# Sorting the values of batches 1 to 3 as rows in four array tiles, by way of DRAM

## The chip, the cores and the metric

The kernel runs on one core of one Trainium2 chip. The metric is the time of one execution on the device in microseconds (us), the median of several runs. The core has TensorE (PE in the profile; its weight loads are PEld), VectorE (DVE), ScalarE (ACT), GpSimd (POOL), SyncE (SP), and 16 DMA engines that all queues share.

## The reference

Sorted attention over blocks, then a feed-forward network. There are 4 batches, 8 heads, 768 positions, 64 values per head; a sequence has 8 blocks of 96.

```python
P = sort_net                                   # [4, 8, 8, 8]
for _ in range(5):
    P = exp(P - max(P, -1));  P = P / (sum(P, -1) + 1e-9);  P = P / (sum(P, -2) + 1e-9)
k_sorted = einsum('bhij,bhjcd->bhicd', P, k_b) # k in blocks: j, position c in the block, d
v_sorted = einsum('bhij,bhjcd->bhicd', P, v_b)
attn = softmax(q_b @ k_sorted.T / 8)           # each block of q against its own sorted block
x = (attn @ v_sorted), heads side by side      # [3072, 512]
r = maximum(x @ w_in, 0)                       # w_in [512, 2048]
out = (s * r * r + b) @ w_out                  # w_out [2048, 512]
```

## The kernel before

Work goes by batch. A batch has two tiles (halves) of 384 tokens for the feed-forward part. `ffn1(t)` computes the hidden layer of tile t: eight steps, each with 8 matmuls of 384 columns (`hps`, L408) into a pair of PSUM banks, a ReLU on ScalarE (`rt`, L422) and a square on VectorE (`gt`, L423). `ffn2(t)` computes the output: three groups of 128 tokens, each with 16 matmuls of 512 columns (`ops`, L433), then scale and bias on VectorE (`ot`, L454) and a store from SP's queue (L457). A fourth of such a group, four matmuls, is a slot; after each slot other work can be put in by a dictionary, `slots`, so the order on TensorE is written out by hand. A tile has 12 slots, 0 to 11.

The attention of batch n = b + 1 is put between the matmuls of `ffn2` of batch b. Its pieces are `K` (`k_piece`, `tp`, L252: sorted keys), `V` (`v_piece`, `tv`, L302: sorted values), `SC` (`s_piece`, `sc`, L317: scores, with the exponential to `at` on ScalarE), `P` (`p_piece`, `pv`, L352: weighted values, divided on VectorE into `x`) and `TD` (`t_dma`, L389: transpose of `x` into `xt` by DMA from SP's queue, for the next `ffn1`). Each piece takes a pair of PSUM banks from a pool of three (`psa`). `q_dma` (L294) transposes the queries by DMA from SP's queue, in two halves of 4 blocks.

The two halves z of a block's 48 positions each lie on rows of their own: a raw tile has a partition for each (head h, block j, half z), and on it 48 positions of 64 values. The sort is a matmul over (h, j, z) with the matrix `PD` (the entries of P, masked). For the scores the sorted keys must have d on the partitions, which comes out of the matmul if the raw data are the stationary operand. For the weighted values the sorted values (`VS`) must have the positions c on the partitions: `v_piece` takes for each d the raw values of 48 positions (filled up to 64) as the stationary operand, and `PD` for one half z as the moving one. To have the 48 positions side by side, the raw values are first copied with c and d exchanged (`VP`): by ScalarE for batch 0, by eight GpSimd copies for the later batches (`v_sort`, L171). So each later batch has 4 pieces with 32 matmuls of 64 columns each:

```python
nc.tensor.matmul(out=ps[z * GAP:(z + 1) * GAP, d, :],
                 lhsT=VP[b % 2][:, d0 + d, :], rhs=PD[b][:, :, z, :],
                 start=True, stop=True)
```

The loads of batch n+1 (`loads`: k, v, then eight DMAs for q, and `v_sort`) are issued on GpSimd's queue; for batch 1 after the loads of the weights, for batches 2 and 3 behind a small copy (`gate`, L558) that waits for the first square of `ffn1` of the batch before. Batch 0's attention and the five rounds of normalising `sort_net` run ahead of all this, up to about 24 us; `ffn1` of batch 0 starts there.

Of the kernel before, what the change touches and what calls it, by code (L numbers as in the profile page):

```python
# [22 lines left out]
def kernel(  # L23
# [32 lines left out]

    raw = [t.rearrange("b h (j z c) d -> b (h j z) (c d)", j=NB, z=2) for t in (q, k, v)]

    const = ctx.enter_context(tc.tile_pool(name="const", bufs=1))
    rawp = ctx.enter_context(tc.tile_pool(name="rawp", bufs=2))  # L60
    trp = ctx.enter_context(tc.tile_pool(name="trp", bufs=2))
# [5 lines left out]
    osb = ctx.enter_context(tc.tile_pool(name="osb", bufs=3))  # L67
    psa = ctx.enter_context(tc.tile_pool(name="psa", bufs=3, space=bass.MemoryType.PSUM))
    psb = ctx.enter_context(tc.tile_pool(name="psb", bufs=2, space=bass.MemoryType.PSUM))
    ctx.enter_context(tc.manual_schedule())  # L70


# [11 lines left out]
    def load(t, b, parts=1):  # L84
        ti = rawp.tile([128, C2, D], BF, tag=f"raw{t}", name=f"raw{t}")
        RAW[t, b] = ti
        n = C2 // parts
        for c in range(0, C2, n):
            nc.gpsimd.dma_start(out=ti[:, c:c + n, :].rearrange("p c d -> p (c d)"),
                                in_=raw["qkv".index(t)][b][:, c * D:(c + n) * D])  # L90

    QTOK = {}

    def load_q(b, ns=range(NB)):
# [4 lines left out]
        for n in ns:  # L99
# [5 lines left out]
    VP = [const.tile([128, D, GAP], BF, name=f"vp{i}") for i in range(2)]  # L105
    KS = [const.tile([128, NG, 2, GAP], BF, name=f"ks{i}") for i in range(2)]
    VS = [const.tile([KR, 2 * NG, VW], BF, name=f"vs{i}") for i in range(2)]
    nc.vector.memset(VP[0][:, :, C2:GAP], 0.0)
    nc.vector.memset(KS[0][:, :, :, C2:GAP], 0.0)
    nc.vector.memset(sne[:, NB, :], 1e-9)  # L110

# [3 lines left out]
    idv = ident.rearrange("p (a e j z) -> p a e j z", a=NHP, e=2, j=NB)  # L115
    emat = const.tile([BH, B, 128], FP)
    nc.gpsimd.memset(emat, 0.0)
    nc.gpsimd.affine_select(out=emat, in_=emat, pattern=[[-H, B], [-1, H], [0, 2 * NB]], base=0,
                            channel_multiplier=1, compare_op=ALU.not_equal, fill=1.0)
    load("k", 0, 3)  # L120
    load_q(0, range(HB))
# [27 lines left out]
    def fill_vs(i):  # L149
        nc.gpsimd.memset(VS[i][:, :, D:VW], 1.0)  # L150
        nc.gpsimd.memset(VS[i][32:GAP, :, D:VW], 0.0)
        nc.gpsimd.memset(VS[i][32:C2, :, D:VW], 1.0)

    fill_vs(0)
    Z = []

    def warm(n, w=512):
# [4 lines left out]
                             start=True, stop=True)  # L162


    def permute(eng, b, src, cs=slice(0, C2), ds=slice(0, D)):
        o = VP[b % 2][:, ds, cs]
        i = src[:, cs, ds].rearrange("p c d -> p d c")
        if eng is nc.scalar:
            eng.copy(out=o, in_=i)
        else:  # L170
            eng.tensor_copy(out=o, in_=i)  # L171


    rstat = const.tile([BH, NB], FP)
    rrec = const.tile([BH, NB], FP)
    jsel = const.tile([128, NB], FP)
    bm = const.tile([128, 2 * 2 * NHP], FP)
    idle = [
        lambda: nc.vector.tensor_reduce(
            out=jsel, in_=ident.rearrange("p (h j z) -> p j h z", h=H, j=NB), axis=AX.XY, op=ALU.add),  # L180
# [8 lines left out]
    for it in range(5):  # L189
        nc.scalar.activation(out=sn, in_=sn, func=AF.Exp)  # L190
        if it >= 1:
            permute(nc.scalar, 0, v0f, slice((it - 1) * CV, it * CV))
# [7 lines left out]
        nc.vector.tensor_reduce(out=rstat, in_=sne.rearrange("p i j -> p j i"),  # L200
                                axis=AX.X, op=ALU.add)
# [17 lines left out]
    def take_p(b0, n, pe):  # L219

        bs = slice(b0, b0 + n)
        tmp = rtp.tile([128, n * NB, NB], FP, tag=f"tmp{n}", name="tmp")
        nc.vector.tensor_tensor(out=tmp, in0=pe.rearrange("p b i j -> p (b i) j"),
                                in1=spread(jsel, [[0, n * NB], list(jsel.ap[1])]), op=ALU.mult)
        nc.vector.tensor_reduce(out=PT[:, bs].rearrange("p b i -> p (b i)"), in_=tmp, axis=AX.X,
                                op=ALU.add)
        cs = rtp.tile([128, n], FP, tag=f"cs{n}", name="cs")
        nc.vector.tensor_reduce(out=cs, in_=PT[:, bs], axis=AX.X, op=ALU.add)
        nc.vector.reciprocal(out=RC[:, bs], in_=cs)

    def build_pd(b):
        pd = const.tile([128, 2, 2, NG], BF, name=f"pd{b}")
        nc.vector.scalar_tensor_tensor(
            out=pd.rearrange("p e z (a i) -> p (e z a) i", i=NB),
            in0=spread(bm, [list(bm.ap[1]), [0, NB]]), scalar=RC[:, b:b + 1],
            in1=spread(PT[:, b], [[0, 4 * NHP], list(PT.ap[2])]), op0=ALU.mult, op1=ALU.mult)
        PD[b] = pd

    def evac(eng, out, in_):
        if eng == "A":  # L240
# [50 lines left out]
    def q_dma(b):  # L291
        qt = q_tile(b)
        for n0 in (0, HB):
            nc.sync.dma_start_transpose(  # L294
                out=qt[:, n0:n0 + HB].rearrange("p n a t -> p (n a) t"),
                in_=QTOK[b][:, n0:n0 + HB].rearrange("p n h d -> p (n h d)"))

    def v_piece(b, d0, eng):
        ps = psa.tile([128, CK, 2 * NG], FP, tag="a", name="tv")
        for d in range(CK):  # L300
            for z in range(2):
                nc.tensor.matmul(out=ps[z * GAP:(z + 1) * GAP, d, :],  # L302
                                 lhsT=VP[b % 2][:, d0 + d, :], rhs=PD[b][:, :, z, :],
                                 start=True, stop=True)
        evac(eng, VS[b % 2][:, :, d0:d0 + CK], ps[0:KR].rearrange("p d g -> p g d"))

# [150 lines left out]
        nc.sync.dma_start(out=out[r0:r0 + 128, ns], in_=ot[:, ns])  # L457


    take_p(0, 1, spread_p(0, 1))  # L460
    build_pd(0)

    nc.gpsimd.tensor_copy(out=ones[:, 0:1], in_=PD[0][:, 0, 0, 0:1])
# [31 lines left out]
    nc.gpsimd.memset(sel, 0.0)  # L495
    for r in range(0, 128, 32):
        nc.gpsimd.memset(sel[r:r + 1], 1.0)
    nc.gpsimd.memset(VP[1][:, :, C2:GAP], 0.0)
    nc.gpsimd.memset(KS[1][:, :, :, C2:GAP], 0.0)
    fill_vs(1)  # L500
    for t, src in ((s_bc, moe_s), (b_bc, moe_b)):
        nc.gpsimd.dma_start(out=t, in_=src.to_broadcast([128, 1]))

    def v_sort(b):
        for i in range(8):
            permute(nc.gpsimd, b, RAW["v", b], ds=slice(i * 8, (i + 1) * 8))

    def loads(b):
        load("k", b)
        load("v", b)  # L510
        load_q(b)
        v_sort(b)

    loads(1)

# [22 lines left out]
    def V(b, i, eng): return lambda: v_piece(b, i * CK, eng)  # L538
# [73 lines left out]
```

## Time and profile before

| | |
|---|---|
| median of 3 runs | 228.4 us (228.14 to 228.75) |
| profiled execution | 228.41 us, span 226.6 us, granted clock 1.00 |
| TensorE busy | 218.9 us |
| VectorE, ScalarE, GpSimd busy | 124.5, 99.5, 68.2 us |
| `hps` and `ops` (L408, L433) | 85.7 us each |
| `tv` (L302), all batches | 512 matmuls, 10.0 us busy |
| GpSimd copies to `VP` (L171) | 24, 19.0 us |
| `vs<-tv` out of PSUM | VectorE 1222 ns, ScalarE 1019 ns each |
| DMA packets | 53930; 44944 of them under 512 bytes |
| q's loads | 32 DMAs, 96 KB each, 9.5 us to landing |

A row of the groups reads: line, engine, operation, output <- input, partitions x elements and type, x count, then busy time, mean ns of one and idle time ahead of it with what ended it. A matmul's duration has its way through the array in it, so the distance of two is shorter than the duration of one. The chain in order of time gives start, length and what ran. In a line of DMA queues the numbers are packets, MB and the packets' time as a share of 16 engines; the share can be over 100%, since packets overlap.

### The profile page before, as it was taken

How to read it: one execution, taken by the hardware profiler on the slowest of the kernel's cores; microseconds unless marked ns; L12 is line 12 of the kernel's file. 1: busy time of each engine (PE TensorE's matmuls, PEld its weight loads, DVE VectorE, ACT ScalarE, POOL GpSimd, SP SyncE). 2: the span in 40 equal slices, each digit the busy share in tenths (PEclk: the TensorE clock that was granted, in tenths of full speed). 3: DMA queues.
4: the chain of work that ended last, by engine and by line, in shares of the span. 5: the costliest groups of instructions: out<-in, count | busy, mean ns of one | idle time of the engine just before them, and what ended most of it. 6: DMA issues, size and time to landing. Idle time of an engine off the chain costs nothing.

```text
span 226.6 us, 5806 instructions
## 1 busy us (share of the span) xinstructions
PE 218.9 (97%) x2542; PEld 133.2 (59%) x2542; DVE 124.5 (55%) x223; ACT 99.5 (44%) x128; POOL 68.2 (30%) x112
## 2 busy tenths in 40 slices
PE   7996999999999999999999999999999999999993
PEld 8985656655555556665555556655566566654452
DVE  6766467553647634498656634498557543441121
ACT  4966476564325225637143236627152246550000
POOL 8467797338400009291000028490000000000000
PEclk9999999999999999999999999999999999999999
DMA  5999999999711558993112459991123240001212
GB/s 190 238 105 133 181 164 206 207 196 136 164 49 49 129 151 136 188 166 72 49 47 73 138 120 176 176 171 36 49 95 67 100 114 0 4 0 46 94 49 93
DMA packets 53930, 25.82 MB, mean 114 GB/s; under 512 B 44944, under 2 KB 49296, under 8 KB 53904
## 3 DMA queue, kind: packets, MB, share of 16 engines
q0 software_dynamic: 30864, 12.85, 47.1%
q1 hardware_dynamic: 23040, 12.59, 20.9%
q8 instruction: 20, 0.33, 0.6%
q14 instruction: 6, 0.05, 0.1%
HBM read 27.27 MB, written 6.29 MB: 148 GB/s over the span
## 4 chain that ended last, share of the span: by engine, by line
PE 86%; DVE 5%; DMA 3%; POOL 2%; ACT 1%; issue 1%; POOLq 0%
PE ops L433 36%; PE hps L408 36%; PE pv L352 3%; PE tv L302 3%; DMA qtok<-in_q_dram 3%; PE sc L317 2%; PE tp L252 2%; PE ops L446 2%; POOL wi L131 1%; DMA sne<-in_sort_net_dram 1%; ACT rt L422 1%; POOL qtok L100 1%; ACT sne L190 1%; PE scb L332 1%; DVE rstat L200 0%
## 5 line engine op out<-in xcount | busy, mean ns | idle before, releaser
L408 PE MATMUL hps<-xt,wi 128*128 128x384 bf16 x512 | 85.7, 326 | 0.3 <-DMA qtok<-in_q_dram 0.3
L433 PE MATMUL ops<-wo,gt 128*128 128x512 bf16 x368 | 85.7, 379 | 0.0
L422 ACT ACTIVATE rt<-hps 128x768 bf16<-128x768 f32 x64 | 51.1, 811 | 53.4 <-PE hps L408 45.6
L423 DVE TENSOR_TENSOR gt<-rt 128x768 bf16<-128x768 bf16 x64 | 46.9, 739 | 41.2 <-ACT rt L422 40.4
L408 PEld LDWEIGHTS <-wi 128*128 128x128 bf16 x512 | 49.3, 98 | 33.5 <-issue 0.6
L433 PEld LDWEIGHTS <-gt 128*128 128x128 bf16 x368 | 33.7, 98 | 36.9 <-issue 0.6
L454 DVE SCALAR_TENSOR_TENSOR ot<-ops,s_bc,bias 128x512 f32<-128x512 f32 (+1 forms) x25 | 18.2, 730 | 30.8 <-PE ops L433 28.2
L322 ACT ACTIVATE at<-sc 112x768 bf16<-112x768 f32 x28 | 21.3, 808 | 30.3 <-PE sc L317 30.3
L100 POOL DMA_DIRECT2D qtok<-in_q_dram x32 | 24.9, 793 | 18.4 <-DMA rawv<-in_v_dram 9.0
L360 DVE TENSOR_TENSOR x<-pv,rec 96x512 bf16<-96x512 f32 x32 | 22.0, 687 | 1.1
L243 DVE CAST vs<-tv 112x1024 bf16<-112x1024 f32 x11 | 13.2, 1222 | 10.8 <-PE tv L302 10.7
L171 POOL COPY vp<-rawv 128x384 bf16<-128x384 bf16 x24 | 19.0, 849 | 0.0
L558 POOL COPY gate<-gt 128x1 bf16<-128x1 bf16 x2 | 0.4, 193 | 56.6 <-DVE gt L423 56.6
L352 PEld LDWEIGHTS <-at 112*128 112x128 bf16 (+1 forms) x256 | 12.8, 101 | 7.2 <-ACT at L322 1.1
L352 PE MATMUL pv<-vs,at 112*128 112x66 bf16 (+1 forms) x256 | 13.9, 195 | 1.0 <-DVE vs L243 1.0
L161 PE MATMUL z<-zeros 128*128 128x140 bf16 (+1 forms) x132 | 11.7, 256 | 1.2 <-DVE zeros L104 1.2
L302 PEld LDWEIGHTS <-vp 128*64 128x64 bf16 x512 | 9.0, 113 | 3.9 <-issue 3.6
L161 PEld LDWEIGHTS <-zeros 128*128 128x128 bf16 x132 | 10.1, 111 | 1.4 <-DVE zeros L103 1.0
L302 PE MATMUL tv<-pd,vp 128*64 128x64 bf16 x512 | 10.0, 197 | 0.9 <-issue 0.8
L241 ACT CAST ks<-tp 128x1024 bf16<-128x1024 f32 x8 | 8.1, 1012 | 4.0 <-PE tp L252 3.9
L131 POOL DMA_DIRECT2D wi<-in_moe_w_in_dram x16 | 8.6, 552 | 2.6 <-DMA wi<-in_moe_w_in_dram 0.9
L241 ACT CAST vs<-tv 112x1024 bf16<-112x1024 f32 x5 | 5.1, 1019 | 9.3 <-PE tv L302 9.3
(76 smaller groups left out, 104.3 us busy)
## 6 DMA issues: line engine op xcount, KB each, us to landing
out_dram<-ot SPq DMA_DIRECT2D x23, 256.0 KB, 2.0
qtok<-in_q_dram POOLq DMA_DIRECT2D x32, 96.0 KB, 9.5
rawk<-in_k_dram POOLq DMA_DIRECT2D x3, 768.0 KB, 6.8
rawv<-in_v_dram POOLq DMA_DIRECT2D x3, 768.0 KB, 10.0
wi<-in_moe_w_in_dram POOLq DMA_DIRECT2D x16, 128.0 KB, 5.2
wo<-in_moe_w_out_dram POOLq DMA_DIRECT2D x4, 512.0 KB, 10.8
v0f<-in_v_dram SPq DMA_DIRECT2D x4, 384.0 KB, 4.3
rawk<-in_k_dram POOLq DMA_DIRECT2D x3, 256.0 KB, 7.9
```

The source lines that it names most:

```text
L100: nc.gpsimd.dma_start(out=QTOK[b][:, n], in_=qv[:, n])
L161: nc.tensor.matmul(out=Z[0][:, 0:w], lhsT=zeros[:, 0:128], rhs=zeros[:, 0:w], start=True, stop=True)
L171: eng.tensor_copy(out=o, in_=i)
L302: nc.tensor.matmul(out=ps[z * GAP:(z + 1) * GAP, d, :], lhsT=VP[b % 2][:, d0 + d, :], rhs=PD[b][:, :, z, :], start=True, stop=True)
L322: nc.scalar.activation(out=at, in_=sc[0:KR, :, 0:TG], func=AF.Exp, scale=scale)
L352: nc.tensor.matmul(out=pv[0:m, e, n * VW:(n + 1) * VW], lhsT=atf[:, c0:c0 + m], rhs=VS[b % 2][:, e * NG + g0 + n, :], start=True, stop=True)
L360: nc.vector.tensor_tensor(out=x[:, :, hp * 128:(hp + 1) * 128].rearrange("p n (e d) -> p e n d", e=2), in0=pvv[:, :, :, 0:D], in1=rec.unsq ...
L408: nc.tensor.matmul(out=H1[i][:, f, 0:TG], lhsT=wi[:, hp, fc:fc + 128], rhs=xt[:, :, hp, :], start=(hp == 0), stop=(hp == NHP - 1))
L422: nc.scalar.activation(out=rt, in_=h, func=AF.Relu)
L423: nc.vector.tensor_tensor(out=gt[:, 2 * i:2 * i + 2, :], in0=rt, in1=rt, op=ALU.mult)
L433: nc.tensor.matmul(out=ops, lhsT=gt[:, f, m * 128:(m + 1) * 128], rhs=wo[:, f, :], start=(f == 0), stop=(f == NF - 1))
L454: nc.vector.scalar_tensor_tensor(out=ot[:, ns], in0=ops, scalar=s_bc, in1=BIAS[0][:, ns], op0=ALU.mult, op1=ALU.add)
```

## The change

For batches 1 to 3, `v_piece` and the GpSimd copies go. The raw k and v tiles of these batches get the order (z, h, j) on the partitions, each loaded by two DMAs of 64 partitions. A new `v_rows` takes a small matrix `PV` (64 rows of one half z by 64 sorted (e, a, i)) as the stationary operand and the raw values themselves, eight positions of 64 values, as the moving one: for each of two parities y of the position and two halves z, one matmul in one of four 64 x 64 tiles of the array. Three pieces of four matmuls make a batch. The result has (y, head and block) on the partitions and the positions along them, the wrong way round for the weighted values. So it goes to a DRAM tile `DV` as rows (48 positions of each half z by 64 sorted heads and blocks, 64 bf16 values = 128 bytes apiece), by two DMAs per piece on SP's queue, and comes back by `v_back`, two DMAs on GpSimd's queue, into `VS` with the positions on the partitions. Masks for the new order are made in `ffn1(1)`.

In the slots, V moves from 5 and 9 to 0 of the first tile, with `v_back` behind it; K from 2 to 3; the scores of the first half from 9 and 11 to 10 and 11; the weighted values of the first half from slot 11 on, one at a time, to slots 3 and 5 of the second tile, in pairs; its transpose from 2 to 5; the second half likewise follows in pairs, its transpose in slot 10 in place of 8. For batch 1, `q_dma` comes behind V in place of ahead of `ffn2`. Half of the filling of `emat` comes later in GpSimd's order.

```diff
+    def load_z(t, b):
+        ti = rawp.tile([128, C2, D], BF, tag=f"raw{t}", name=f"raw{t}")
+        RAW[t, b] = ti
+        for z in range(2):
+            nc.gpsimd.dma_start(out=ti[z * 64:(z + 1) * 64].rearrange("p c d -> p (c d)"),
+                                in_=rawz["qkv".index(t)][b, z])
...
+    DV = drp.tile([BLK, 2 * NG, D], BF, name="dv")
+    VO = const.tile([128, 2, C2 // 2, D], BF)
...
-    nc.gpsimd.affine_select(out=emat, in_=emat, pattern=[[-H, B], [-1, H], [0, 2 * NB]], base=0,
+    nc.gpsimd.affine_select(out=emat[:, 0], in_=emat[:, 0], pattern=[[-1, H], [0, 2 * NB]], base=0,
...
+    def masks_z():
+        idz = ident.rearrange("p (z a e j) -> p z a e j", z=2, a=NHP, e=2)
+        nc.vector.tensor_reduce(
+            out=jselz, in_=ident.rearrange("p (z h j) -> p j z h", z=2, h=H), axis=AX.XY, op=ALU.add)
+        nc.vector.tensor_reduce(
+            out=bmz.rearrange("p (e z a) -> p e z a", e=2, z=2),
+            in_=idz.rearrange("p z a e j -> p e z a j"), axis=AX.X, op=ALU.add)
+        bv = bmz.rearrange("p (e z a) -> p e z a", e=2, z=2)
+        nc.vector.tensor_tensor(out=bmv.rearrange("p (e a) -> p e a", e=2), in0=bv[:, :, 0],
+                                in1=bv[:, :, 1], op=ALU.add)
...
     def build_pd(b):
+        PD[b] = build(b, bmz if b else bm, "pd").rearrange("p (e z a) i -> p e z (a i)", e=2, z=2)
+        if b:
+            PV[b] = build(b, bmv, "pv").rearrange("p m i -> p (m i)")
...
+    def v_rows(b, i, eng):
+        src, n = RAW["v", b], 8
+        ps = psa.tile([128, 2, n, D], FP, tag="a", name="vo")
+        for y in range(2):
+            for z in range(2):
+                zs, ys = slice(z * 64, (z + 1) * 64), slice(y * 64, (y + 1) * 64)
+                c0 = i * 2 * n + y
+                nc.tensor.matmul(out=ps[ys, z], lhsT=PV[b][zs], rhs=src[zs, c0:c0 + 2 * n - 1:2, :],
+                                 start=True, stop=True, tile_position=(z * 64, y * 64))
+        vo = VO[:, :, i * n:(i + 1) * n, :]
+        evac(eng, vo.rearrange("p z c d -> p z (c d)"), ps.rearrange("p z c d -> p z (c d)"))
+        dv = DV.rearrange("(z t c y) g w -> z t (y g) c w", z=2, y=2, c=n)
+        for z in range(2):
+            nc.sync.dma_start(out=dv[z, i], in_=vo[:, z])
+
+    def v_back(b):
+        for z in range(2):
+            nc.gpsimd.dma_start(out=VS[b % 2][z * GAP:z * GAP + C2, :, 0:D],
+                                in_=DV[z * C2:(z + 1) * C2])
...
-    def v_sort(b):
-        for i in range(8):
-            permute(nc.gpsimd, b, RAW["v", b], ds=slice(i * 8, (i + 1) * 8))
...
     def loads(b):
-        load("k", b)
-        load("v", b)
+        load_z("v", b)
+        load_z("k", b)
         load_q(b)
-        v_sort(b)
...
-    ffn1(1, {-2: [TP(0, 1, 2, "D")], 1: [lambda: take_p(1, B - 1, PB), PDB(1)], 4: [PDB(2)],
+    ffn1(1, {-2: [TP(0, 1, 2, "D")], 1: [masks_z, lambda: take_p(1, B - 1, PB, jselz), PDB(1)], 4: [PDB(2)],
...
-        q_dma(n)
+        if b:
+            q_dma(n)
         s0 = {
-            2: [K(n, 0, "A"), K(n, 1, "D"), K(n, 2, "A")],
-            5: [V(n, 0, "D"), V(n, 1, "A"), V(n, 2, "D")],
-            9: [V(n, 3, "D"), SC(n, 0, 0), SC(n, 0, 1)],
-            11: [P(n, 0, 0), SC(n, 0, 2), SC(n, 0, 3)]}
+            0: [V(n, 0, "D"), V(n, 1, "A"), V(n, 2, "D"), lambda: v_back(n)]
+               + ([] if b else [lambda: q_dma(n)]),
+            3: [K(n, 0, "A"), K(n, 1, "D"), K(n, 2, "A")],
+            10: [SC(n, 0, 0), SC(n, 0, 1)],
+            11: [SC(n, 0, 2), SC(n, 0, 3)]}
         ffn2(2 * b, s0)
-        ffn2(2 * b + 1, {0: [P(n, 0, 1)], 1: [P(n, 0, 2)],
-                         2: [P(n, 0, 3), TD(n, 0), SC(n, 1, 0), SC(n, 1, 1)],
-                         4: [P(n, 1, 0)], 5: [P(n, 1, 1), SC(n, 1, 2), SC(n, 1, 3)],
-                         7: [P(n, 1, 2)], 8: [P(n, 1, 3), TD(n, 1)]})
+        ffn2(2 * b + 1, {3: [P(n, 0, 0), P(n, 0, 1)],
+                         5: [P(n, 0, 2), P(n, 0, 3), TD(n, 0)],
+                         6: [SC(n, 1, 0), SC(n, 1, 1)], 7: [SC(n, 1, 2), SC(n, 1, 3)],
+                         8: [P(n, 1, 0), P(n, 1, 1)],
+                         10: [P(n, 1, 2), P(n, 1, 3), TD(n, 1)]})
```

More of the change, by code (lines that the diff above doesn't have):

```diff
@@ L57 @@
     raw = [t.rearrange("b h (j z c) d -> b (h j z) (c d)", j=NB, z=2) for t in (q, k, v)]
+    rawz = [t.rearrange("b h (j z c) d -> b z (h j) (c d)", j=NB, z=2) for t in (q, k, v)]
     const = ctx.enter_context(tc.tile_pool(name="const", bufs=1))
@@ L69 @@
     psb = ctx.enter_context(tc.tile_pool(name="psb", bufs=2, space=bass.MemoryType.PSUM))
+    drp = ctx.enter_context(tc.tile_pool(name="drp", bufs=1, space=bass.MemoryType.DRAM))
     ctx.enter_context(tc.manual_schedule())
@@ L104 @@
     nc.vector.memset(zeros[:, 128:512], 0.0)
-    VP = [const.tile([128, D, GAP], BF, name=f"vp{i}") for i in range(2)]
+    VP = const.tile([128, D, GAP], BF)
     KS = [const.tile([128, NG, 2, GAP], BF, name=f"ks{i}") for i in range(2)]
     VS = [const.tile([KR, 2 * NG, VW], BF, name=f"vs{i}") for i in range(2)]
-    nc.vector.memset(VP[0][:, :, C2:GAP], 0.0)
+    DV = drp.tile([BLK, 2 * NG, D], BF, name="dv")
+    VO = const.tile([128, 2, C2 // 2, D], BF)
+    nc.vector.memset(VP[:, :, C2:GAP], 0.0)
     nc.vector.memset(KS[0][:, :, :, C2:GAP], 0.0)
@@ L147, in load_w @@
             nc.gpsimd.dma_start(out=wo[:, fs, :], in_=wov[:, fs, :])
[L149 to L154, printed above, removed]
+    nc.gpsimd.memset(VS[0][:, :, D:VW], 1.0)
+    nc.gpsimd.memset(VS[0][32:GAP, :, D:VW], 0.0)
+    nc.gpsimd.memset(VS[0][32:C2, :, D:VW], 1.0)
+    for z in range(2):
+        em = emat[:, 1:B, z * 64:(z + 1) * 64]
+        nc.gpsimd.affine_select(out=em, in_=em, pattern=[[-H, B - 1], [-1, H], [0, NB]], base=-H,
+                                channel_multiplier=1, compare_op=ALU.not_equal, fill=1.0)
     Z = []
@@ L162, in warm, with permute @@
                              start=True, stop=True)
[L165 to L171, printed above, removed]
+    def permute(cs):
+        nc.scalar.copy(out=VP[:, :, cs], in_=v0f[:, cs, :].rearrange("p c d -> p d c"))
     rstat = const.tile([BH, NB], FP)
@@ L177 @@
     bm = const.tile([128, 2 * 2 * NHP], FP)
+    jselz = const.tile([128, NB], FP)
+    bmz = const.tile([128, 2 * 2 * NHP], FP)
+    bmv = const.tile([128, 2 * NHP], FP)
     idle = [
@@ L191 @@
         if it >= 1:
-            permute(nc.scalar, 0, v0f, slice((it - 1) * CV, it * CV))
+            permute(slice((it - 1) * CV, it * CV))
         if it in (1, 2):
@@ L217, in spread_p, with take_p @@
         return pe
-    def take_p(b0, n, pe):
+    def masks_z():
[8 more added lines that the diff above has]
+                                in1=bv[:, :, 1], op=ALU.add)
+    def take_p(b0, n, pe, sel):
         bs = slice(b0, b0 + n)
@@ L223, in take_p @@
         nc.vector.tensor_tensor(out=tmp, in0=pe.rearrange("p b i j -> p (b i) j"),
-                                in1=spread(jsel, [[0, n * NB], list(jsel.ap[1])]), op=ALU.mult)
+                                in1=spread(sel, [[0, n * NB], list(sel.ap[1])]), op=ALU.mult)
         nc.vector.tensor_reduce(out=PT[:, bs].rearrange("p b i -> p (b i)"), in_=tmp, axis=AX.X,
@@ L229, in take_p, with build @@
         nc.vector.reciprocal(out=RC[:, bs], in_=cs)
-    def build_pd(b):
[L232 to L237, printed above, removed]
+    PV = {}
+    def build(b, m, name):
+        n = m.shape[1]
+        pd = const.tile([128, n, NB], BF, name=f"{name}{b}")
+        nc.vector.scalar_tensor_tensor(
+            out=pd, in0=spread(m, [list(m.ap[1]), [0, NB]]), scalar=RC[:, b:b + 1],
+            in1=spread(PT[:, b], [[0, n], list(PT.ap[2])]), op0=ALU.mult, op1=ALU.mult)
+        return pd
+    def build_pd(b):
+        PD[b] = build(b, bmz if b else bm, "pd").rearrange("p (e z a) i -> p e z (a i)", e=2, z=2)
+        if b:
+            PV[b] = build(b, bmv, "pv").rearrange("p m i -> p (m i)")
     def evac(eng, out, in_):
@@ L296, in q_dma @@
                 in_=QTOK[b][:, n0:n0 + HB].rearrange("p n h d -> p (n h d)"))
+    def v_rows(b, i, eng):
[13 more added lines that the diff above has]
+    def v_back(b):
+        for z in range(2):
+            nc.gpsimd.dma_start(out=VS[b % 2][z * GAP:z * GAP + C2, :, 0:D],
+                                in_=DV[z * C2:(z + 1) * C2])
     def v_piece(b, d0, eng):
@@ L302, in v_piece @@
                 nc.tensor.matmul(out=ps[z * GAP:(z + 1) * GAP, d, :],
-                                 lhsT=VP[b % 2][:, d0 + d, :], rhs=PD[b][:, :, z, :],
+                                 lhsT=VP[:, d0 + d, :], rhs=PD[b][:, :, z, :],
                                  start=True, stop=True)
@@ L457, in store @@
         nc.sync.dma_start(out=out[r0:r0 + 128, ns], in_=ot[:, ns])
-    take_p(0, 1, spread_p(0, 1))
+    take_p(0, 1, spread_p(0, 1), jsel)
     build_pd(0)
@@ L497 @@
         nc.gpsimd.memset(sel[r:r + 1], 1.0)
-    nc.gpsimd.memset(VP[1][:, :, C2:GAP], 0.0)
     nc.gpsimd.memset(KS[1][:, :, :, C2:GAP], 0.0)
-    fill_vs(1)
+    nc.gpsimd.memset(VS[1][:, :, D:VW], 1.0)
+    nc.gpsimd.memset(VS[1][32:GAP], 0.0)
+    nc.gpsimd.memset(VS[1][32:C2, :, D:VW], 1.0)
     for t, src in ((s_bc, moe_s), (b_bc, moe_b)):
         nc.gpsimd.dma_start(out=t, in_=src.to_broadcast([128, 1]))
-    def v_sort(b):
-        for i in range(8):
-            permute(nc.gpsimd, b, RAW["v", b], ds=slice(i * 8, (i + 1) * 8))
     def loads(b):
-        load("k", b)
-        load("v", b)
+        load_z("v", b)
+        load_z("k", b)
         load_q(b)
-        v_sort(b)
     loads(1)
@@ L537, in K, with V @@
     def K(b, i, eng): return lambda: k_piece(b, i * CK, eng)
-    def V(b, i, eng): return lambda: v_piece(b, i * CK, eng)
+    def V(b, i, eng): return lambda: v_rows(b, i, eng)
     def SC(b, h, i): return lambda: s_piece(b, h, i)
```

## The prediction

> **What bounds the kernel now.** I read the busy table first, then the chain that ended last, by line and in order of time, then the DMA views, because the change adds DMA.
>
> ```profile
> PE 218.9 (97%) x2542; PEld 133.2 (59%) x2542; DVE 124.5 (55%) x223; ACT 99.5 (44%) x128; POOL 68.2 (30%) x112
> ...
> PE 86%; DVE 5%; DMA 3%; POOL 2%; ACT 1%; issue 1%; POOLq 0%
> PE ops L433 36%; PE hps L408 36%; PE pv L352 3%; PE tv L302 3%; DMA qtok<-in_q_dram 3%; PE sc L317 2%; PE tp L252 2%; PE ops L446 2%; POOL wi L131 1%; DMA sne<-in_sort_net_dram 1%; ACT rt L422 1%; POOL qtok L100 1%; ACT sne L190 1%; PE scb L332 1%; DVE rstat L200 0%
> ```
>
> TensorE works 97% of the span and the chain is TensorE's own work: from 52 us on it has no wait. What is taken off TensorE there shortens the run by as much, and a wait put in front of it lengthens it by as much. In order of time, the stage of batch 2 and, above it, one row from the stage before:
>
> ```profile
> 47.75 0.98 PE cps L527 x16
> ...
> 102.30 2.59 PE ops L433 x12
> 104.89 1.64 PE tp L252 x96
> 106.53 2.70 PE ops L433 x12
> 109.23 1.64 PE tv L302 x96
> 110.86 3.56 PE ops L433 x16
> 114.42 0.63 PE tv L302 x32
> 115.05 0.45 PE sc L317 x16
> 115.49 1.83 PE ops L433 x8
> 117.33 0.27 PE pv L352 x8
> ```
>
> A slot is four `ops` matmuls, 2.59/3 = 0.863 us. The sort of the values (`tv`) takes 1.64 + 0.63 = 2.27 us per batch.
>
> **Removed from TensorE:** three times 2.27 = 6.8 us (batch 0 keeps its sort). **Put in its place:** 12 matmuls of 64 rows by 64 columns with 512 moving columns per batch. The trace has no such tile, but it has the two halves of it: `cps` puts 16 matmuls of 512 columns in four column tiles into 0.98 us, 61 ns each where `ops` takes 216 ns, so four column tiles run at once; `sc` puts 16 matmuls of 96 columns in two row tiles into 0.45 us, 28 ns each, where 96 columns at `ops`' rate (512 in 216 ns) take 40 ns, so row tiles overlap too. Bounds: 12 x 61 ns = 0.74 us, and 12 x 216 ns = 2.59 us. I take 0.74, since `cps` has the same columns. Saving: 3 x (2.27 - 0.74) = **4.6 us**. The K, score and weighted-value matmuls keep their number; pairing them only moves them.
>
> The Trainium skill ("TensorEngine Tiling (Array Packing)", Key Properties) says that a change of tiling mode drains the array; the group after a change takes 2.70 instead of 2.59 us here. Both kernels change in and out of tiles at each group, so by the rule as by the row the sum moves by under 0.2 us a batch.
>
> **Removed elsewhere, worth nothing:** 24 GpSimd copies (19.0 us, 849 ns each). While they run, one `gt` operation of VectorE stretches to some 4 us (ScalarE waits 3.97 us at 103.2), but `hps` keeps its 20.80 us per 128 matmuls, as TensorE has three PSUM buffers ahead. One of four evacuations per batch also goes. **Added on VectorE** in the second FFN tile: two mask reductions (0.27 us by the `bm` row), one small product, three further builds (0.35 us by the `pd` row), at most 1.8 us over several steps. They delay squares, and three `rt` buffers at 1.3 us a step (3.9 us) cover that; uncovered it would cost about 1 us. The split `emat` select runs in GpSimd's 4.8 us wait for `pd`. Loading k and v in two halves moves the same bytes.
>
> **The round trip through DRAM** decides. Per batch SP issues 6 stores of 1024 pieces of 128 bytes, and GpSimd, once they have landed, 2 loads of 3072 pieces; the first weighted values wait for the loads. Behind the stores on SP's queue stand the output stores, and in the first turn the two transposes of q. Behind the loads on GpSimd's queue stand only loads for later. No store of 128-byte pieces to DRAM is in the trace. The nearest rows: one microsecond full of q's load (256 bytes read, 128 written), and one full of SP's transposes (256-byte packets out of SBUF):
>
> ```profile
> q0 software_dynamic: 1223, 0.15, 241.1%
> ```
>
> ```profile
> q1 hardware_dynamic: 830, 0.21, 115.2%
> ```
>
> So 0.82 us per 1000 packets in the first and 1.20 us in the second. The first is nearer in size, the second in queue and source; I take the middle, 1.01 us per 1000, 6.2 us for 6144. Times below count from the start of the first `ops` group of a stage (102.30 above).
>
> - Stores: slot 0 ends at 0.9, the first piece's matmuls at 1.1 and, with a tail of 0.2 us (an `ops` matmul lasts 379 ns at 216 ns spacing), at 1.3. VectorE is free of the last `gt` (ScalarE 0.81, VectorE 0.56) at 1.4. The evacuation takes 1.22 us (`vs<-tv`), so the first store goes at 2.7 and the third piece's at 3.9. An output store lands 2.0 us after issue with some 0.7 us of data, so 1.3 us go by around it; from the transposes I take 1.3 us ahead of the data and 0.5 us after it. Data: 4.0 to 10.2, last landing 10.7; the first half's last store lands 1.0 us earlier, at 9.7. SP's issuing (0.33 us for an output store, 1.44 us for a transpose of 1536 packets, so up to 1.0 us for 1024 pieces) ends at 8.7 at the latest and lies beside the data.
> - Loads: issuing costs GpSimd 779 ns at 768 pieces (q) and 566 ns at 128 (k, v), 0.33 ns a piece, so 0.52 + 3072 x 0.33 ns = 1.5 us (in plain proportion 3.1). Then 1.3 us to first data, 6144 pieces at q's rate 5.0 us, and 1.0 us to landing. From 9.7: **18.5 us**. Bounds: with half of q's bytes read per piece 2.5 us less, with issue in proportion 2.2 us more.
> - Needed: slot 3 of the second tile, after 16 slots (13.8 us), sort 0.7, K 1.6, four scores 1.8 and 0.3 for changes of mode: **18.3 us**. The move from slot 11 of the first tile to there is the cover; without those four slots the wait would be 3.5 us longer.
>
> So TensorE waits 0.2 us in each of the last two stages. In the first stage the transposes of q follow the stores: 10.2 + 1536 packets at 830/us (1.9) + 0.5 = 12.6, against scores due at slot 10: 11 x 0.863 + 0.7 + 1.6 + 0.2 = 12.0. That is 0.6 us of wait, which also gives the values their time. Waits: 0.6 + 0.2 + 0.2 = **1.0 us**. What comes later keeps a margin: the transpose of the first half (x) starts at slot 5 and has 6 slots and other work, 8.6 us, for some 2 us of normalising and 3.7 us to land. An output tile has three buffers, so 12 slots of 0.86 us pass before one is wanted again.
>
> **Sum:** the profiled execution took 228.41 us (span 226.6), which is the median of the runs (228.4). 228.4 - 4.6 + 1.0 = **224.8 us**.
>
> A rule of the Trainium skill speaks against the change: "DMA: Bandwidth & Descriptors", Specifications, says that transfers under 512 bytes are read, modified and written. Read so, each stored piece would move twice, 12.4 us in place of 6.2, and by it the time would be about 243 us. The same page ("Why small descriptors are slow") counts, for a packet, one cycle per 32 bytes plus 3, which for 128 bytes is an estimate of 8 ns per engine, 3.2 us for the stores, and the time 223.8 us. The q row has 128-byte writes, to SBUF, that are not slowed in that way; no run shows it for DRAM.
>
> **Rivals.**
>
> *Fully hidden, 223.8 us.* The stores go at q's rate (5.0 us) or the loads at half its time; then both waits vanish. For it: q's load is bound by twice the bytes per piece. Chance 0.17.
>
> *Slower: the stores' landing.* Every microsecond d that they take beyond 6.2 us is paid three times, as the stage has no slack left at slot 3. The waits are 1.0 + 3d, and pass the 4.6 us saved at d = 1.2 us, that is from 7.4 us for 6144 pieces, 830 per us: just the transposes' rate. At 600 per us (10.2 us, d = 4.0) the time is 223.8 + 13.0 = 236.8 us; at 400 (15.4 us, d = 9.2) it is 252.4 us. For it: SP's only measured rate for small packets is the point of balance, and writing DRAM in small pieces has no row. Against it: output stores of 2 KB land in 2.0 us. The return leg too can add d. Chance 0.38, of which 0.06 lie within 0.7 us of no change.
>
> *The four tiles do not overlap.* Then the sort takes 2.59 us, 0.3 more than now: 228.4 + 1.0 + 1.0 = 230.4 us. Against it are `cps` and `sc`; that no row has both kinds of tile at once is for it. Chance 0.07.
>
> *Forecast:* almost hidden, 224.3 to 227.6, chance 0.36. That leaves 0.02 for a cause not seen, counted as slower.
>
> **Numbers.** No change means within 0.3%, 0.7 us, about what a measurement of this kernel can tell. Faster: 0.36 + 0.17 = 0.53; same 0.06; slower 0.32 + 0.07 + 0.02 = 0.41. The range goes from 223.4 (hidden, and a little of the tiles' overlap better than counted) to 240, where the stores run at about 540 per us; I leave 0.14 above it and 0.03 below. The forecast's own range is 224.3 to 227.6.
>
> **What would show it.** In the chain after: `vo` groups of about 0.7 us where `tv` had 2.27; a wait of `pv` for the DMA of `vs` of about 0.2 us in the last two stages, and of `sc` for `qt` of about 0.6 us in the first; `dv` stores landing about 8 us after the first issue. A wait of `pv` over 1.5 us per stage, or `vo` over 1.5 us, would make the forecast wrong, the first by the rate of the stores or of the loads, which the packets per microsecond on the two queues tell apart.

## The result, and the profile after

The changed kernel takes 250.79 us (median of 4 runs, 249.47 to 253.03), the kernel before beside it 228.27 us: a ratio of 1.099 (95% interval 1.091 to 1.108), 22.5 us slower. The forecast was 224.8 us, 3.5 us faster.

From the page of the changed kernel, the busy times and the chain that ended last, by engine and line (span 249.3 us):

```profile
PE 220.6 (88%) x2194; PEld 128.4 (51%) x2194; DVE 110.0 (44%) x226; ACT 99.5 (40%) x128; POOL 63.3 (25%) x101
...
PE 63%; DMA 21%; DVE 6%; issue 3%; SPq 2%; ACT 2%; POOLq 0%; POOL 0%; DVEq 0%
PE hps L462 33%; PE ops L487 19%; DMA vs<-dv 15%; DMA dv<-VO 5%; PE pv L406 4%; SPq L344 2%; PE ops L500 1%; PE sc L371 1%; PE tv L356 1%; DVE VO L275 1%; ACT rt L476 1%; DMA sne<-in_sort_net_dram 1%; ACT sne L202 1%; PE z L175 1%; DVE vs L275 0%
```

Where the kernel before had 86% of its chain on TensorE and 3% on DMA, a fifth of it is now DMA, most of it the loads back (`vs<-dv`). TensorE's busy time did not fall, although 348 matmuls are gone. The chain in order of time for the stage of batch 2 shows the turn of it:

```profile
113.02 0.86 PE ops L487 x4
113.88 0.77 PE vo L338 x12
114.65 2.71 PE ops L487 x12
...
118.02 4.86 DMA dv<-VO
...
124.91 10.75 DMA vs<-dv
...
135.79 1.09 PE pv L406 x16
136.89 3.41 PE ops L487 x8
```

`vo` takes 0.77 us where `tv` had 2.27. The stage begins at 113.0. The stores land at 122.9, 9.9 us into it. The second load back, issued at 124.9, lands at 135.66. The two lines after it are slow too: `pv` takes 1.09 us where two pieces had 0.54, and eight `ops` matmuls 3.41 where they had 1.73. The timeline of TensorE gives the wait ahead of `pv` in brackets:

```profile
80.59 1.09 PE L406 MATMUL pv<-vs,at 112*128 112x66 bf16 x16 [10.22 <-DMA vs<-dv]
135.79 1.09 PE L406 MATMUL pv<-vs,at 112*128 112x66 bf16 x16 [5.24 <-DMA vs<-dv]
192.11 1.09 PE L406 MATMUL pv<-vs,at 112*128 112x66 bf16 x16 [5.02 <-DMA vs<-dv]
```

And the busy times by stretch (columns: length, then busy time of PE, PEld, DVE, ACT and POOL, then the granted clock, the DMA share and GB/s) show why the work after a wait is slow:

```profile
131.00:138.00 7.00, 2.21 (x20) 1.41 (x21) 1.82 (x5) 0.00 (x0) 0.00 (x0) 0.76 0.67 107
138.00:140.00 2.00, 2.00 (x6) 0.72 (x5) 0.22 (x1) 0.00 (x0) 0.00 (x0) 0.50 0.00 0
140.00:142.00 2.00, 2.00 (x21) 1.28 (x19) 1.12 (x4) 0.00 (x0) 0.00 (x0) 0.65 0.00 0
142.00:150.00 8.00, 8.00 (x95) 4.58 (x94) 5.28 (x11) 2.99 (x4) 0.00 (x0) 1.00 0.36 84
```

During the wait the granted clock falls to 0.50, and it is back at 1.00 only some time after TensorE has work again: 2.8 us in the first stage, 5.6 in the second and 4 in the third. So the account is: saved on the sort 3 x (2.27 - 0.77) = 4.5 us; waits of `pv` 10.2 + 5.2 + 5.0 = 20.4; a wait of the scores 0.3; and from the first `pv` of a stage to the next hidden layer 11.6, 13.0 and 12.2 us, where the same work adds up to 10.2 us at full clock, so 6.2 us. Together 26.9 - 4.5 = 22.4 us.

### The profile page after: what moved, and what is told of

Same layout as the page of the kernel before. It is cut to its first block, busy times and chain, and to the rows that moved or that the text cites. A ratio compares the mean times of both kernels' runs of the same rounds, so it can differ in the third digit from the quotient of the medians.

```text
span 249.3 us, 5152 instructions
## 1 busy us (share of the span) xinstructions
PE 220.6 (88%) x2194; PEld 128.4 (51%) x2194; DVE 110.0 (44%) x226; ACT 99.5 (40%) x128; POOL 63.3 (25%) x101
## 4 chain that ended last, share of the span: by engine, by line
PE 63%; DMA 21%; DVE 6%; issue 3%; SPq 2%; ACT 2%; POOLq 0%; POOL 0%; DVEq 0%
PE hps L462 33%; PE ops L487 19%; DMA vs<-dv 15%; DMA dv<-VO 5%; PE pv L406 4%; SPq L344 2%; PE ops L500 1%; PE sc L371 1%; PE tv L356 1%; DVE VO L275 1%; ACT rt L476 1%; DMA sne<-in_sort_net_dram 1%; ACT sne L202 1%; PE z L175 1%; DVE vs L275 0%
## 5 line engine op out<-in xcount | busy, mean ns | idle before, releaser
L487 PE MATMUL ops<-wo,gt 128*128 128x512 bf16 x368 | 89.5, 393 | 0.0
L487 PEld LDWEIGHTS <-gt 128*128 128x128 bf16 x368 | 35.0, 101 | 41.4 <-issue 5.9
L477 DVE TENSOR_TENSOR gt<-rt 128x768 bf16<-128x768 bf16 x64 | 35.5, 558 | 45.4 <-ACT rt L476 45.1
L349 POOL DMA_DIRECT2D vs<-dv x6 | 8.0, 1341 | 39.6 <-DMA dv<-VO 39.6
L413 DVE RECIPROCAL rec<-pv 96x8 f32<-96x8 f32 x32 | 6.3, 198 | 20.9 <-PE pv L406 20.9
L175 PE MATMUL z<-zeros 128*128 128x140 bf16 (+1 forms) x132 | 11.6, 254 | 1.2 <-DVE zeros L114 1.2
L371 PEld LDWEIGHTS <-ks 64*128 64x128 bf16 x224 | 5.2, 94 | 5.7 <-issue 4.1
L371 PE MATMUL sc<-qt,ks 64*128 64x96 bf16 x224 | 7.4, 204 | 0.4 <-DMA qt<-qtok 0.3
L275 DVE CAST VO<-vo 128x1024 bf16<-128x1024 f32 x6 | 7.1, 1217 | 0.7 <-PE vo L338 0.7
## 6 DMA issues: line engine op xcount, KB each, us to landing
wo<-in_moe_w_out_dram POOLq DMA_DIRECT2D x4, 512.0 KB, 11.2
```

What stands on the lines that cost most here:

```text
L175: nc.tensor.matmul(out=Z[0][:, 0:w], lhsT=zeros[:, 0:128], rhs=zeros[:, 0:w], start=True, stop=True)
L275: nc.vector.tensor_copy(out=out, in_=in_)
L371: nc.tensor.matmul(out=sc[:, e, n * BLK:(n + 1) * BLK], lhsT=KS[b % 2][pr, g0 + n].rearrange("p z c -> p (z c)"), rhs=QT[b][pr, half * HB ...
L477: nc.vector.tensor_tensor(out=gt[:, 2 * i:2 * i + 2, :], in0=rt, in1=rt, op=ALU.mult)
L487: nc.tensor.matmul(out=ops, lhsT=gt[:, f, m * 128:(m + 1) * 128], rhs=wo[:, f, :], start=(f == 0), stop=(f == NF - 1))
```

## The experiments

The theory after the first look was that only the return leg is wrong: all else is the gain that was forecast. The rivals for why it is long were the uneven addresses of its pieces (A), GpSimd's queue (B), other transfers beside it (C), the number of small pieces (D), a slow source (E), and that a load reaches 48 partitions of one half of SBUF alone (F).

**No loads back.**

```diff
-            0: [V(n, 0, "D"), V(n, 1, "A"), V(n, 2, "D"), lambda: v_back(n)]
+            0: [V(n, 0, "D"), V(n, 1, "A"), V(n, 2, "D")]
```

> Leaves out the loads back from DRAM: the weighted values of batches 1 to 3 read values that were never brought in. Theory (the return leg is what is late, all else is a gain): no wait of pv for the DMA of vs, no fall of TensorE's clock, and the sort's saving stands alone, 228.3 - 3 x (2.27 - 0.77) = 223.8 us; the wait of the scores for qt in the first stage (0.3 us) may stay, so 223.5 to 224.5. Rival (the four tiles, the stores or the new slots cost something themselves): over 226 us.

Measured: 225.14 us against 229.11 for the kernel before beside it, ratio 0.980 (0.974 to 0.986). Everything but the return leg is worth 4 us. In its profile the scores of the first stage wait 2.5 us for `qt`, more than the 0.3 expected, and a little over a microsecond after the wait the granted clock goes down (last column but two):

```profile
66.21 0.72 PE L371 MATMUL sc<-qt,ks 64*128 64x96 bf16 x16 [2.50 <-DMA qt<-qtok]
```

```profile
67.00:68.00 1.00, 1.00 (x4) 0.20 (x2) 0.00 (x0) 1.00 (x2) 0.00 (x0) 0.78 1.15 317
68.00:69.00 1.00, 1.00 (x18) 0.74 (x18) 0.75 (x1) 0.72 (x2) 0.00 (x0) 0.50 0.73 277
```

**The slots alone**, in the kernel before: scores in slots 10 and 11, weighted values in pairs from slot 3 of the second tile, and nothing else.

> The kernel before with only the later slots for the scores, weighted values and transposes of x (the fourth piece of the values stays in slot 9). Theory (slots are free, as TensorE has the same work and nothing waits for the later pieces): 228.3 us, within 0.7. Rival (the transpose of x lands too late for the next hidden layer, or pairs wait for PSUM): 1 us or more per batch, over 231 us, with a wait of hps for xt or of pv for x.

Measured: 229.54 against 229.11 us, ratio 1.001 (0.998 to 1.005), with no wait on TensorE over 0.2 us. The later slots cost nothing.

**Even addresses.**

```diff
-    VS = [const.tile([KR, 2 * NG, VW], BF, name=f"vs{i}") for i in range(2)]
+    VS = [const.tile([KR, 2 * NG, 80], BF, name=f"vs{i}")[:, :, 0:VW] for i in range(2)]
```

> The changed kernel with rows of VS 160 bytes apart in place of 132, so that each piece of 128 bytes begins on a multiple of 32 bytes; four buffers for the exponentials in place of six make the room. Theory A (pieces at uneven addresses of the destination are slow): the loads' data take about 5 us in place of 9 to 10, the wait of pv in the last two stages falls from 5 us to 1 and with it the clock's fall goes, so about 250.8 - 2 x (4 + 2) - some 6 in the first stage = 233 us. Theory B (how GpSimd's queue serves these loads, 32 pieces in a packet one after another, is slow) and theory C (they share the engines with other transfers): 250.8 us, unchanged within 1.5.

Measured: 248.97 us, ratio 1.085 (1.075 to 1.095); waits of `pv` 10.2, 4.1 and 3.9 us. Theory A is worth about 1 us a stage in two stages, not the 4 that it had promised.

**SP's queue for the loads.**

```diff
-            nc.gpsimd.dma_start(out=VS[b % 2][z * GAP:z * GAP + C2, :, 0:D],
+            nc.sync.dma_start(out=VS[b % 2][z * GAP:z * GAP + C2, :, 0:D],
```

> The changed kernel with the two loads back issued on SP's queue in place of GpSimd's, same addresses. Theory A (uneven addresses): the data take about 9 us as before and the time stays at 250.8 within 2 us. Theory B (GpSimd's queue): the data go at the rate of the stores on SP's queue, 1140 pieces per us, 5.4 us, the wait of pv falls to about 1 us in the last two stages, and the time to some 235 us. Theory C (sharing with the transposes of q in the first stage): on SP's queue the loads stand behind the transposes, so only the first stage gets shorter, by up to 7 us.

Measured: 248.82 us, ratio 1.084 (1.077 to 1.092). TensorE's timeline:

```profile
76.68 0.82 PE L371 MATMUL sc<-qt,ks 64*128 64x96 bf16 x16 [9.66 <-DMA qt<-qtok]
...
136.15 1.06 PE L406 MATMUL pv<-vs,at 112*128 112x66 bf16 x16 [3.22 <-DMA vs<-dv]
```

In the last two stages the wait falls to 3.2 and 3.4 us, but the pieces go at about 750 per us on this queue too (1502 in the two us from 129), so theory B is not the main reason. Some 2 us of each of these stages do go with the queue and its issuing: the second load lands 20.7 us into the stage, against 22.6 in the changed kernel. In the first stage the wait only changes its owner: q's transposes now stand behind the loads.

**Unbroken rows.** The loads write 8 KB in one piece per partition; the number of bytes, the source, queue and partitions stay.

```diff
-            nc.gpsimd.dma_start(out=VS[b % 2][z * GAP:z * GAP + C2, :, 0:D],
-                                in_=DV[z * C2:(z + 1) * C2])
+            nc.gpsimd.dma_start(out=VS[b % 2][z * GAP:z * GAP + C2].rearrange("p g w -> p (g w)")[:, 0:2 * NG * D],
+                                in_=DV[z * C2:(z + 1) * C2].rearrange("t g w -> t (g w)"))
```

> The changed kernel with the loads back written as one unbroken row of 8 KB per partition, over the columns of ones too, in place of 64 pieces of 128 bytes 132 bytes apart: same bytes, same source, same queue, same partitions (its weighted values are not the reference's). Theory D (each small piece has a cost at its destination): the data take 3 us or less in place of 9, no wait of pv and no fall of the clock in the last two stages, so about 250.8 - 2 x (5.1 + 2) = 236.5 us, and down to 226 if the first stage's wait goes too. Rival E (the source is slow: rows of DRAM just written, or few engines): data still about 9 us, time within 2 us of 250.8.

Measured: 231.3 us against 228.8, ratio 1.008 (1.003 to 1.013): 19 of the 22 us are gone.

```profile
68.23 0.71 PE L371 MATMUL sc<-qt,ks 64*128 64x96 bf16 x16 [3.83 <-DMA qt<-qtok]
...
124.33 0.69 PE L406 MATMUL pv<-vs,at 112*128 112x66 bf16 x16 [0.59 <-DMA vs<-dv]
...
173.70 0.69 PE L406 MATMUL pv<-vs,at 112*128 112x66 bf16 x16 [0.71 <-DMA vs<-dv]
```

Theory D holds: the cutting of the load into small pieces is what makes the return long, and the source is not slow (E falls). The data take some 4 us, though, and not under 3.

**One load of 112 partitions**, pieces as before, with 16 rows of zeros between the halves:

```diff
-        for z in range(2):
-            nc.gpsimd.dma_start(out=VS[b % 2][z * GAP:z * GAP + C2, :, 0:D],
-                                in_=DV[z * C2:(z + 1) * C2])
+        nc.gpsimd.dma_start(out=VS[b % 2][:, :, 0:D], in_=DV)
```

> The changed kernel with the rows of both halves, and 16 rows of zeros between them, in one load of 112 partitions in place of two loads of 48. Theory F (a load to 48 partitions of one half of SBUF reaches only some of the paths into it, as q's load to 96 partitions does not): 7168 pieces at q's 1220 per us, 5.9 us, the wait of pv in the last two stages 2 us, with little fall of the clock: about 250.8 - 2 x (3 + 2) - a part of the first stage's 10 us = 238 us. Rival D (each piece costs the same wherever it lands): 7168 at some 700 per us, 10.2 us, wait 6 us, time 251 to 255 us.

Measured: 247.31 us, ratio 1.080 (1.072 to 1.089); waits of `pv` 5.0, 5.6 and 5.1 us. The first line below is GpSimd's queue over two us of the changed kernel, the second that of this one; a packet holds up to 32 pieces there:

```profile
q0 software_dynamic: 59, 0.18, 115.8%
```

```profile
q0 software_dynamic: 75, 0.31, 101.5%
```

At 128 bytes a piece that is 0.18 MB / 128 / 2 = 700 pieces per us against 1210. These two rows are the later part of one load and the early part of the other. From the first packet to the last, 6144 pieces take 9.1 us in the changed kernel (675 per us) and 7168 take some 8 us here (890 per us), so F holds, with a factor of about 1.3. It brought little, as there is one issue of 2.47 us, and the first packets come after it; with two issues of 1.34 us the first half's data move beside the second issue.

**Two queues at once**, GpSimd's for one half and SP's for the other:

> The changed kernel with the first half's load on GpSimd's queue and the second half's on SP's, so that both halves of SBUF are written at once. Theory F: both loads in some 5 us, the wait of pv in the last two stages down to 1 to 2 us, about 238 us, less what q's transposes lose behind the load in the first stage. Rival D: the two share the engines, the last lands as late as before, 248 to 251 us.

Measured: 249.42 us, ratio 1.089 (1.079 to 1.100). `pv` waits 3.8 and 4.2 us, and in the first stage the scores wait 11.2 us for `qt`, behind the load on SP's queue. The time is the one expected under D; the waits of `pv` lie between the two expectations. But the two loads hardly moved at once: SP's data ran from 126.1 to 129.7 us, GpSimd's from about 129.0 on. So the run says little on F. It shows something else: SP's load alone began at 841 pieces in half a microsecond and fell to about 350, with the same pieces, partitions and queue, and nothing beside it. The loads of the changed kernel do the same, some 1500 pieces in their first microsecond and 600 to 770 per us after it. Neither D nor F explains this fall, and no run here does.

**The sort earlier**, in the hidden layer ahead of the stage (batches 2 and 3):

```diff
-            ffn1(2 * b + 1, {})
+            ffn1(2 * b + 1, {2: [V(n, 0, "D")], 4: [V(n, 1, "D")],
+                             6: [V(n, 2, "D"), lambda: v_back(n)]} if n < B else {})
```

> The changed kernel with the value sort of batches 2 and 3 put into the second hidden-layer tile ahead of its stage (steps 2, 4 and 6), so that the round trip starts some 6 us earlier; batch 1 is left as it was. Theory (the return leg is late by 5 us and nothing else is wrong): no wait of pv and no fall of the clock in the last two stages, 250.8 - 2 x (5.1 + 2) = 236.5 us, what is left being the first stage. Rival (the pieces take PSUM from the hidden layer, or the stores share the engines with the loads of q): hps waits, or pv still waits, time over 240 us.

Measured: 251.24 us, ratio 1.090 (1.079 to 1.102). The expectation failed: the loads went out at 3.9 us of the stage in place of 10.6, 6.7 us sooner, but landed 20.7 and 23.2 us into it, where the changed kernel had 22.6, with waits of 4.1 and 6.7 us. In its chain a load takes 15.4 us, and 18.1 in the last stage:

```profile
119.54 15.42 DMA vs<-dv
```

The reason is what moves at the same time: now the transposes of q of every batch fall on the loads, as in the changed kernel they do in the first stage. There, in the two us from 66, both queues carry little:

```profile
q0 software_dynamic: 27, 0.11, 90.0%
q1 hardware_dynamic: 295, 0.08, 79.2%
```

That is about 150 packets of transposes and 430 pieces per us together, where transposes alone went at 830 and loads alone at 700 to 1050.

**Transposes first.** In the changed kernel, for batch 1, the first half of q's transposes goes ahead of the stores on SP's queue.

```diff
...
-        if b:
-            q_dma(n)
+        q_dma(n, (0, HB) if b else (0,))
...
-               + ([] if b else [lambda: q_dma(n)]),
+               + ([] if b else [lambda: q_dma(n, (HB,))]),
...
```

> The changed kernel with one thing moved: for batch 1 the first half of q's transposes goes ahead of the stores of the values in SP's queue, the second half stays behind them. Theory (in the first stage the transposes and the loads back share the engines and slow each other, which is why its wait is 10 us and not 5): the wait of sc for qt goes (0.3 us), and with half of the transposes out of the way the wait of pv falls to about 7 us, so 247 us. Rival (the transposes have no part in it): the wait stays at 10 us, or grows by the 1 us that the stores are held up, 250 to 252 us.

Measured: 248.83 us, ratio 1.083 (1.072 to 1.094), and the wait of the first stage falls from 10.2 to 6.2 us. Theory C holds for the first stage: the transposes and the loads slow each other. It is not what makes the loads long in the last two stages: in the eight us from 126 of the changed kernel SP's queue moved 22 packets, 0.05 MB, beside 207 and 0.74 MB on GpSimd's; in those from 182 7 beside 213.

**Whole rows through DRAM.** To have unbroken loads and keep the columns of ones, the rows in DRAM carry the columns of ones: 66 values in one kernel, 80 in another. Both have the transposes first and the first weighted values in slot 4.

```diff
...
-    DV = drp.tile([BLK, 2 * NG, D], BF, name="dv")
+    VR = 66
+    DV = drp.tile([BLK, 2 * NG, VR], BF, name="dv")
...
-        evac(eng, vo.rearrange("p z c d -> p z (c d)"), ps.rearrange("p z c d -> p z (c d)"))
+        evac(eng, vo[:, :, :, 0:D], ps)
...
```

> The rows in DRAM get the columns of ones too, 66 values, 132 bytes a piece, so that the loads back are unbroken rows of 8448 bytes on both sides; the stores become pieces of 132 bytes at uneven addresses. For batch 1 the first half of q's transposes goes ahead of the stores, and the first weighted values move from slot 3 to 4. Theory D (small pieces at the destination are what is slow): if the stores keep 1140 pieces per us, no wait of pv and none of sc for qt, no fall of the clock: 228.5 - 4.5 = 224 us, up to 226. Rival (pieces of 132 bytes at uneven addresses in DRAM are slower to store): the stores land later, at half the rate by 5.4 us; pv then waits 3 to 4 us per stage and the time is 236 to 244 us.

> As the kernel with rows of 66 values, but with 80: pieces of 160 bytes that begin on multiples of 32 bytes, loads of 10240 bytes a row, the columns past 64 filled with ones ahead. Theory D: as there, 224 to 226 us, whether uneven addresses matter or not. If the one with 66 is slow and this one is not, the uneven addresses in DRAM are the reason; if both are slow, any store or load in this order is.

Measured: with 66 values 269.09 us, ratio 1.172 (1.164 to 1.180); with 80 values 237.0 us, ratio 1.028 (1.019 to 1.037). With 66 the store of a piece of 132 bytes is what is slow. SP's queue over one us of stores in the changed kernel, and over two us with 132 bytes:

```profile
q1 hardware_dynamic: 1144, 0.14, 93.2%
```

```profile
q1 hardware_dynamic: 631, 0.08, 178.0%
```

1144 pieces per us against 316. With 160 bytes the stores start at about 1100 and end at 800 per us, but the two loads of 48 partitions together move their 0.98 MB in 5.9 us, 167 GB/s (145 in the middle of it), and `pv` waits 5.1, 1.4 and 2.1 us in the profiled run, which took 238.5 us. So the first part of theory D's expectation, 224 to 226 us, failed.

**Whole rows in one load** of 112 partitions, all else as with 80 values:

> The kernel with rows of 80 values, and all rows, 16 of zeros between the halves among them, in one load of 112 partitions and 10 KB each. Theory F (a load to one half's 48 partitions reaches only some of the paths into SBUF): 1.15 MB at over 300 GB/s, 3.5 us, where the two loads of 0.98 MB took 6 us; landing some 6 us after issue, no wait of pv in the last two stages (1.4 and 2.1 us), 2 to 3 us of wait in the first in place of 5; about 229.4 - 4.5 + 2.5 + 1 = 228.5 us, 227 to 231. Rival (the load is bound by DRAM or by what else moves): still 6 us or more for the data, pv waits 2 us or more in each stage, 236 us or more.

Measured: 231.99 us against 229.08, ratio 1.010 (1.007 to 1.014); waits 4.4, 0.4 and 1.0 us. The last two stages are mended; the first waits 4.4 us, where 2 to 3 were expected.

**The hybrid.** Batch 1 keeps the sort of the kernel before; batches 2 and 3 go through DRAM in whole rows and one load.

```diff
...
+        nc.gpsimd.dma_start(out=VB[b % 2].rearrange("p g w -> p (g w)"),
+                            in_=DV.rearrange("t g w -> t (g w)"))
...
+        if b == 1:
+            load("k", b)
+            load("v", b)
+            load_q(b)
+            for i in range(8):
+                ds = slice(i * 8, (i + 1) * 8)
+                nc.gpsimd.tensor_copy(out=VP[:, ds, 0:C2], in_=RAW["v", b][:, :, ds].rearrange("p c d -> p d c"))
+            return
...
```

> As the kernel with one load of whole rows, but batch 1 keeps the sort of the kernel before, with its GpSimd copies; only batches 2 and 3 go by way of DRAM. In their stages q's transposes are done before the stores begin. Theory (what the change saves on TensorE is 1.5 us per batch, and what it lost was the return leg, the clock after the wait, and the transposes of q in the first stage): no wait in the last two stages, 229.0 - 2 x 1.5 = 226 us, ratio 0.985 to 0.99, faster than both. Rival (the return leg is still late): waits of pv of over 1.5 us in these stages, ratio at 1 or above.

Measured: 227.1 us against 229.08, ratio 0.990 (0.987 to 0.993), faster than both kernels. Its TensorE timeline, and two us from the middle of a load on GpSimd's queue: from 124 in the kernel with 80 values, which has two loads of rows, then from 117 in the hybrid, which has one:

```profile
120.95 0.69 PE L407 MATMUL pv<-vs,at 112*128 112x66 bf16 x16 [0.32 <-DMA vs<-dv]
170.09 0.69 PE L407 MATMUL pv<-vs,at 112*128 112x66 bf16 x16 [0.45 <-DMA vs<-dv]
```

```profile
q0 software_dynamic: 43, 0.29, 93.7%
```

```profile
q0 software_dynamic: 66, 0.68, 102.9%
```

0.68 MB in two us is 340 GB/s, against 145 GB/s. The Trainium skill ("SBUF — State Buffer", Door 1: the DMA port swizzle) says that DMA bandwidth goes by how many of 16 ports a transfer's partitions reach and that 64 partitions of one half reach 8; its section "Can I just issue two DMAs to hit both halves?" adds that two transfers are not joined. By these figures, an estimate, one load would go at up to twice the rate. The two rows agree in kind, by a factor of 2.3; over the whole of the loads, 0.98 MB in 5.9 us and 1.15 MB in some 4.2, it is 1.6.

## Why the prediction was wrong

**The sort** was sized right: 0.74 us forecast, 0.77 measured per batch, so four tiles do run at once. **The stores** were too: 6.2 us of data and the last landing at 10.7, against 1144 pieces per us, 5.4 us, and 9.9. The rival of slow stores did not come true: the price that the prediction worked out from the Trainium skill's rule on transfers under 512 bytes ("DMA: Bandwidth & Descriptors", Specifications) was 12.4 us for the data, and pieces that begin on multiples of 128 bytes took 5.4. **The slots** were free, as said.

**The loads back** are the term that failed. "6144 pieces at q's rate 5.0 us" took the rate of a load to 96 partitions for two loads to 48 of one half each, with rows 132 bytes apart; they ran at 1055 pieces per us in the two us from 126 and at 700 after it, 9.1 us from the first packet to the last. The leg was 8.8 us in the forecast, issue to landing, and 12.1 us in the trace (123.6 to 135.7); its bound above, 2.2 us more for the issue, did not cover the rate, for which I gave no bound above at all. It also began 0.9 us later than forecast (10.6 for 9.7), as its wait ended only with the last of the stores. And the values were due earlier, at 17.5 and not 18.3: "four scores 1.8" is twice too much, since 0.45 us in the chain is two pieces of 8 matmuls. So `pv` waited 5 us in place of 0.2. The unbroken rows show that the pieces are the main part (the wait falls to 0.6), and the loads of 112 partitions that the reach of half of SBUF is in it. Why the pieces of one load slow down part way stays open.

**The first stage** failed by a sentence: "which also gives the values their time". The transposes and the loads are not one after the other but at once, and each slows the other. The wait was 10.2 us where 0.6 was forecast.

**The clock** was missing. A wait of 5 us costs 7 to 8 us here, as the work after it runs at 0.5. In the profiles, waits of up to 1.6 us (the sort earlier, 1.58) left it at 1.00. The shortest after which it fell was 2.1 us (80 values, third stage: 0.50 from about 182.2, 1.4 us after work began again), then 2.5 us (no loads back) and 3.2 us (SP's queue, 0.56 in the two us from 136). That makes the rival's "paid three times" too small, and the price a step and not a slope: with values 4.1 us later than forecast (22.6 for 18.5), its own formula gives 223.8 + 1.0 + 12.3 = 237.1 us; 0.8 us less of cover in three stages, the 5 us more of the first stage and 6.2 us of clock bring it to 250.7.

The hybrid returns 2.0 of the 3.0 us that two batches should save. Of the rest, 0.8 us are its two waits. The remainder is within its interval and was not traced.

## What to carry to other kernels

Price each leg of a detour through DRAM by a row with the same side in small pieces, the same span of partitions and the same neighbours on the engines; where no row has all three, the leg needs a bound above, not a middle. A transfer that writes small pieces to SBUF is better turned round: scatter on the DRAM side in aligned pieces, then load whole rows across both halves of SBUF in one DMA. A wait on TensorE is a price of its own length only while it is short; past some 2 us, in these runs, add the clock.

## What the runs showed of the hardware

- Stores of 128-byte pieces to DRAM at aligned addresses ran at 1144 per us, 146 GB/s; pieces of 132 bytes at uneven ones at 316 per us.
- Loads of 128-byte pieces into 48 partitions took 9.1 us for 6144, 675 per us (1055 at first, 700 later), into 112 partitions some 8 us for 7168, 890 per us (970 to 1210 in rows of two us); with rows 160 bytes apart 48 partitions took them 13 to 27% faster than with 132. One load, with nothing beside it, fell from 841 pieces in half a microsecond to about 350; no run shows why.
- Transposes on SP's queue and loads of small pieces on GpSimd's, together, moved less than either alone: a load took 15 to 18 us to land in place of 10 to 11.
- Issuing a load from GpSimd took 0.53 us for 48 whole rows, 1.34 us for 3072 pieces and 2.47 us for 7168, and the data came after it.
- After waits of TensorE of 2.1 us and more the granted clock fell to 0.50 (2.1, 2.5, 3.2 and some 5 to 10 us), up to 1.4 us after work began again; after waits of up to 1.6 us it stayed at 1.00.
